# HGRN2 attention and a GELU block on one core: the first unit's steps in another order, with a new plan behind them

## The chip, the cores and the metric

The kernel runs on one core of a Trainium2 chip. The metric is the device time of one execution in microseconds, as the median over runs. All data are float32.

## The reference

```python
# q, k, v, f_logit: (4, 8, 768, 48)
f = 1.0 / (1.0 + np.exp(-f_logit))
for t in range(S):
    state = f[:, :, t, :, None] * state + np.einsum('bhd,bhe->bhde', k[:, :, t], v[:, :, t])
    y[:, :, t] = np.einsum('bhd,bhde->bhe', q[:, :, t], state)
x = y.transpose(0, 2, 1, 3).reshape(B * S, H * D)     # (3072, 384)
h = x @ w_in                                          # (3072, 2048)
g = h * (1.0 / (1.0 + np.exp(-1.702 * h)))
return g @ w_out                                      # (3072, 384)
```

A gated linear recurrence over 768 tokens for 32 heads of 48 features is followed by a block of two dense layers.

## The kernel before

The tokens are cut into 12 units of U = 256 (three for each batch entry). `attention(n)` makes the steps of unit n; the dense layers' work for the units that are done is a list, `fill`, from which items are emitted between them. A unit is two halves (f = 1 forward, f = 0 backward: the second half is kept with its time reversed) of 128 tokens, in chunks of C = 64. The steps are these:

- `load_raw(n, j)` loads f_logit, q or k (j = 0, 1, 2) into `raw`, in four pieces for units 0 and 1. `turn` puts features on the partitions: for units 0 and 1 by products with `ident` on TensorE (L376, eight to a PSUM bank, two banks for each of f, q, k), which ScalarE copies out (L381). f goes through the sigmoid to `F`, q and k to slots of `X`: KF and KR for k, QF and QR for q.
- `begin_gates` multiplies neighbouring decays to `tot` on GpSimd (L436): decays over 2, 4, ... 64 tokens.
- Six levels, m = 1 to 32, build the masked score matrix of each chunk. At level l, `set_aside` copies k to `Kc` on ScalarE (L514), `score` multiplies (L445, 32 products), `promote` multiplies k's and then q's slots in place by the decays over m tokens on VectorE (L539, two instructions for units 0 and 1), and `evacuate` merges the scores into `A` under masks: VectorE at levels 0 to 4 (L486, L505), ScalarE at level 5 (four copies, L495). q's promotion can start only when the level's products have read q.
- `turn_k` transposes the fully promoted k (L618) and ScalarE copies it to `kn`. `load_v` loads v into `vt` (first half) and `vr` (second half); `reverse_v` reverses vr's tokens by a stream shuffle on VectorE after a load that reverses the blocks of 32.
- Part "S": `add` multiplies A by v into `y` (L555), kn by v gives `pd` (L666), and VectorE carries the state over four chunks in `st`, a product and a sum for each chunk (L691, L692). Part "W": the states times q are added to y (L713), ScalarE copies y to `yT` (L728), and DMAs bring yT into the layout `xT` that the dense layers read (`to_x`, L778 and L783).

The dense layers' products are `h` (L1127, xT times w_in, 256 tokens) and `o` (L1141). The weights come in 16 pairs of 768 KB through `fetch_weights` (L207, into one of three `bits` buffers) and are converted in four steps: a prelu on ScalarE (L239), then `a`, `s` and the write to w_in or w_out on VectorE (L235, L228, L238). Pairs 0, 1 are w_in and 2, 3 are w_out of the first four of the 16 feature blocks, pairs 4, 5 and 6, 7 those of the next four, and so on.

Until unit 2 has ended every engine takes its instructions in the written order. `opening()` writes unit 0 by hand; units 1 to 3 follow `PLAN`, one string of steps behind each part: f an item of the dense layers, c one step of a conversion, w a weight fetch, p the start of the next conversion, k (any other letter) one idle product, s another sum. `keep_up` makes such idle products (L116), whose result nothing reads. From unit 3 on TensorE and GpSimd keep the written order and a scheduler orders the other engines. A DMA's issue waits in its queue until the one eight before it has landed.

The levels in the opening, and the end of it:

```python
for l in range(NL):
    chosen[:] = [2, 3][l % 2:][:1]
    level(l)                      # here: scores, products, promote k, promote q, set_aside
    ...
turn_k(0)
turn_k(2)
for l in range(NL - 1):
    evacuate(l)
    if l == 1:
        units[0][3]()             # reverse_v
```

Of the kernel before, what the change touches and what calls it, by code (L numbers as in the profile page):

```python
# [13 lines left out]
ALU = mybir.AluOpType  # L14
# [9 lines left out]
def kernel(  # L24
# [94 lines left out]
    nc.vector.memset(ones, 1.0)  # L119
    nc.scalar.activation(ones, ones, AF.Sigmoid)  # L120
    nc.vector.memset(A, 0.0)
    nc.vector.memset(ones, 1.0)
    serial = count()
    flat_A = A.rearrange("p c f t -> p (c f t)")
    keep_up(2, 192, (flat_A[:, :P], flat_A[:, :192]))

# [41 lines left out]
    w_in = const.tile([P, NFF // 2, NK, 2 * P], F32, name="w_in")  # L168
    w_out = const.tile([P, NFF, DM], F32, name="w_out")
    k_toks = [tc.dram_tile([2, G, P // 32, 32 * NP], F32, name=f"k_tok{j}") for j in range(2)]  # L170
    D2, DR = 2 * D, P - 2 * D
# [90 lines left out]

    HOLES = {(N_FILL, 0): "ccp", (N_FILL, 1): "cwcc", (N_FILL, 2): "cwp", (N_FILL, 3): "cc", (N_FILL, 4): "cw"}

# [43 lines left out]
    def load_v(n):  # L308


        if n >= NALL:
            return
        b, s0 = n // NU, n % NU * U
        vts[n] = ld.tile([P, 2, DM], F32, tag="vt", name=f"vt_{n}", bufs=2)
        vrs[n] = ld.tile([P, DM], F32, tag="vr", name=f"vr_{n}", bufs=1)
        nc.sync.dma_start(
            out=vts[n][:, 1].rearrange("p (h d) -> p h d", h=H), in_=v[b, :, s0:s0 + HALF, :].rearrange("h p d -> p h d")
        )
        for i in range(4):
            t0 = s0 + U - 32 * (i + 1)  # L320
            nc.sync.dma_start(
                out=vrs[n][32 * i:32 * (i + 1)].rearrange("p (h d) -> p h d", h=H),
                in_=v[b, :, t0:t0 + 32, :].rearrange("h p d -> p h d"),
            )

    def reverse_v(n):

        nc.vector.stream_shuffle(vts[n][:, 0], vrs[n], list(range(31, -1, -1)))

# [8 lines left out]
    def attention(n):  # L338
# [19 lines left out]
        def turn(j, outs, fn=None, pieces=None):  # L358

            if n >= N_FILL:  # L360
                for f in (1, 0):
                    out = outs(f)
                    at, step = (0, 1) if f else (HALF - 1, -1)
                    nc.vector.transpose(  # L364
                        view(out, at, [[HALF, NP], [step, R4], [R4 * step, 32]]),
                        by_half[:, j, f].rearrange("p a (j d) -> p (a j) d", j=R4)[:, :, :32],
                    )
                if fn:
                    fn()
                return  # L370
            for j0 in pieces or range(0, R, 4):
                pt = bank([P, 4, P], f"t_{n}_{j}_{j0}")
                for jj in range(4):
                    for h in range(2):
                        x = (j0 + jj) * D
                        nc.tensor.matmul(  # L376
                            pt[h * HS:(h + 1) * HS, jj, :], lhsT=by_pair[j][:, h, x:x + HS], rhs=ident, start=True, stop=True
                        )
                for f in (1, 0):
                    at, step = (j0, 1) if f else (HALF - 1 - j0, -1)  # L380
                    nc.scalar.activation(  # L381
                        view(outs(f), at, [[HALF, NP], [R * step, 16], [step, 4]]),
                        pt.rearrange("p j (a f i) -> p f a i j", a=NP, f=2)[:, 1 - f],
                        (AF.Tanh if n > 1 else AF.Sigmoid) if fn else AF.Copy, scale=0.5 if fn and n > 1 else 1.0,
                    )
            if fn and n > 1:
                half_up()
# [19 lines left out]

        def begin():
            turn(1, lambda f: slot(query(n, f)))
            if n > N_FILL:  # L410
                load_raw(n + 1, 1)

        def begin_k(between=None):
            turn(2, lambda f: slot((KR, KF)[f]))
# [65 lines left out]

        def evacuate_one(l, c, sc):

# [8 lines left out]
            if m == 32:  # L491
# [7 lines left out]
                return  # L499
            for at, f in ((HS + m, 1), (0, 0)):  # L500
                dims = [[HALF, n_c], [2 * m, 32 // m], [1, m]]
# [22 lines left out]

        def promote(l, q_too=False):

# [4 lines left out]
            if n < N_FILL:  # L531
                nb = nb // 2
                for base, other, at, to in ((KF, KR, 0, m), (QR, QF, 0, m)):
                    f = 1 if base == KF else 0
# [9 lines left out]
            if l + 1 < NL:  # L544
                set_aside(l + 1, q_too)
# [41 lines left out]
        def open_level(l):  # L587
            if l % 2 == 0:
                lane_scores(0, 1) if l == 0 else scores("y" if l == 2 else "sc")
            by_level[l] = t["both"]  # L590
            score(l % 2, l, queries(l))
            promote(l)

        def open_evacuate(l):
            for c, sc in by_level[l]:
                evacuate_one(l, c, sc[:, :, l % 2])

# [56 lines left out]
        def _():  # L654
# [17 lines left out]
            if not n:  # L672
                units[1][0][2]()
                add()

                seen = t["py"][HS:HS + 1, 1, 0, 1, :1]
                nc.scalar.copy(seen, seen)
            if n != N_FILL - 1:
                load_v(n + 1)
# [16 lines left out]
        def _():  # L696
# [26 lines left out]
            def half(h):  # L723
                for g in range(h, NG):
                    for f in (1, 0):
                        at, step = (g * HS, 1) if f else (U - 1 - g * HS, -1)
                        to, of = (rows(h), columns(h, g)) if g else (slice(0, HS + D),) * 2
                        nc.scalar.copy(view(yT[to], at, [[U, NP], [step, HS]]), py[of, g, :, f, :])  # L728
                two = ((nc.scalar, nc.sync), (nc.sync, nc.scalar))[n] if h and n < N_FILL else (nc.sync,)
                to_x(lambda h: (yT[rows(h), :NK], lambda r, d: yT[r:r + d, NK]), xT[:, :, :U], NG, (h,), two)  # L730
# [56 lines left out]

        return (begin_f, begin, begin_k, begin_gates), parts, (open_level, open_evacuate, turn_k), lambda: reverse_v(n)

# [417 lines left out]
    def parts_of(n):  # L1207
# [103 lines left out]
    def opening():  # L1311

        begin_f, begin, begin_k, begin_gates = units[0][0]
        next_f, next_q, next_k, next_gates = units[1][0]
        level, evacuate, turn_k = units[0][2]
# [10 lines left out]
        load_v(0)  # L1326
        load_raw(1, 1)
        fetch_weights()
        fetch_weights()
        for l in range(NL):  # L1330
            chosen[:] = [2, 3][l % 2:][:1]
            level(l)
            if l in (2, 3):
                next_f((0, 4)[l - 2:][:1])
            elif l < NL - 1:
                keep_up(1)
            if l == 1:
                begin_pair(0)
                state["begin"] = 1

        nc.scalar.activation(q_end, q_end, AF.Gelu_apprx_sigmoid)
        chosen[:] = [2, 3]
        turn_k(0)
        turn_k(2)
        for l in range(NL - 1):
            evacuate(l)
            if l == 1:
                units[0][3]()
        chosen[:] = [2, 3, 2, 3]
        next_q()  # L1350
        begin_pair(1)
        state["begin"] = 2
        evacuate(NL - 1)
        units[0][1][-2][1]()
        next_gates()
        for _ in range(NOP):
            convert()
        fetch_weights()

    fill = []  # L1360
    opening()
    FIRST = 'k'
    PLAN = {
# [70 lines left out]
```

## Time and profile before

| | |
|---|---|
| median of three runs | 587.08 us (585.69, 587.08, 596.66) |
| profiled execution | 587.35 us, span 585.4 us |
| TensorE busy | 564.4 us, 96% |
| VectorE, ScalarE, GpSimd busy | 441.0, 288.8, 142.5 us |
| DMA | 60.34 MB, mean 103 GB/s |
| first `h` product of the dense layers | 38.95 us |
| xT of unit 0: first issue, last issue | 33.64, 35.62 us |
| first state product `y` (L713) of unit 1 | 62.24 us |
| first `h` product of unit 1 | 69.36 us |

Times in the trace are microseconds from the start of the span. A line of the timeline gives start, length, engine, source line, operation, written and read tiles, and in brackets the idle time before it with what ended it. A float32 product leaves two records. SPq and ACTq are the instruction queues of SyncE and ScalarE while they issue DMAs.

### The profile page before, as it was taken

The page shows a single profiled execution, that of the slowest core. Times are in us where ns is not written, and L with a number is a line of the kernel's source. Part 1 is how long each engine was busy: PE and PEld are TensorE (multiplying, and loading weights), DVE is VectorE, ACT ScalarE, POOL GpSimd, SP SyncE. Part 2 cuts the span into 40 slices and gives each one's busy share as a digit, 9 for nine tenths or more (in the row PEclk, how much of TensorE's full clock was granted, in tenths as well). Part 3 has the DMA queues.
Part 4 walks back from the last instruction along what each step waited for, and adds up shares of the span by engine and source line. Part 5 has one row for each costly group of instructions (what it writes and reads, how often), then busy time and mean ns, then how long its engine had stood idle before and what let it go on. Part 6 is the DMA issues. An engine that isn't in the chain of part 4 may idle for free.

```text
span 585.4 us, 18532 instructions
## 1 busy us (share of the span) xinstructions
PE 564.4 (96%) x7838; PEld 514.6 (88%) x7838; DVE 441.0 (75%) x697; ACT 288.8 (49%) x588; POOL 142.5 (24%) x226
## 2 busy tenths in 40 slices
PE   7899889999999999999999999999999999999997
PEld 6767667676899999999999999999999999999896
DVE  2898877986888786887796897786897786461284
ACT  4755354323543563564563564563563563652440
POOL 4020220614452602402502502502402403103000
PEclk9999999999999999999999999999999999999999
DMA  7869695833352452453542343442451211001000
GB/s 183 197 185 221 172 241 133 234 79 89 100 143 55 126 125 58 116 128 82 131 113 56 103 128 86 126 115 57 120 130 43 64 39 29 29 2 36 19 1 28
DMA packets 86771, 60.34 MB, mean 103 GB/s; under 512 B 33505, under 2 KB 78465, under 8 KB 86689
## 3 DMA queue, kind: packets, MB, share of 16 engines
q1 hardware_dynamic: 86208, 58.57, 40.0%
q8 instruction: 62, 1.02, 0.7%
q10 hardware_dynamic: 481, 0.59, 0.4%
q14 instruction: 20, 0.16, 0.1%
HBM read 45.49 MB, written 8.91 MB: 93 GB/s over the span
## 4 chain that ended last, share of the span: by engine, by line
PE 73%; DVE 10%; DMA 7%; SPq 4%; ACT 3%; issue 2%; ACTq 0%; DVEq 0%
PE h L1033 17%; PE o_Y L894 14%; PE o_Z L894 9%; PE h_y L1033 6%; PE sc L445 6%; PE o_X L894 5%; PE o_W L894 4%; DMA bits<-in_moe_w_in_dram 3%; PE h L1127 3%; PE o L1141 3%; DVE X L364 2%; PE y L713 2%; PE y L555 2%; PE sc L666 2%; DVE X L543 1%
## 5 line engine op out<-in xcount | busy, mean ns | idle before, releaser
L543 DVE TENSOR_TENSOR X<-X,tot 128x1024 f32<-128x1024 f32 x50 | 67.7, 1354 | 44.7 <-PE sc L445 38.4
L514 ACT COPY Kc<-X 128x512 f32<-128x512 f32 x72 | 48.4, 672 | 81.6 <-DVE X L543 61.2
L995 POOL TENSOR_TENSOR E<-xT 128x128 f32<-128x128 f32 (+1 forms) x36 | 16.0, 455 | 229.4 <-DMA xT<-yT 229.4
L1127 PE MATMUL h<-xT,w_in 128*128 128x256 f32 x288 | 65.9, 383 | 2.6 <-DMA xT<-yT 1.8
L1127 PEld LDWEIGHTS h<-xT,w_in 128*128 128x128 f32 x288 | 53.7, 190 | 12.3 <-issue 2.4
L1033 PE MATMUL h<-E,w_in 128*128 128x128 f32 (+1 forms) x476 | 62.8, 277 | 0.5 <-DVE g L1061 0.5
L1033 PEld LDWEIGHTS h<-E,w_in 128*128 128x128 f32 x476 | 57.4, 192 | 1.4 <-issue 0.8
L894 PE MATMUL o_Y<-T,S 128*128 128x192 f32 x320 | 57.7, 329 | 0.0
L1063 ACT ACTIVATE g<-g 128x512 f32<-128x512 f32 (+1 forms) x70 | 40.4, 590 | 27.1 <-DVE g L1061 26.8
L894 PEld LDWEIGHTS o_Y<-T,S 128*128 128x128 f32 x320 | 52.2, 190 | 0.6
L1061 DVE TENSOR_TENSOR g<-g,h 128x512 f32<-128x512 f32 (+1 forms) x58 | 36.1, 637 | 15.3 <-PE h L1033 14.4
L364 DVE STREAM_TRANSPOSE X<-raw 128x512 f32<-128x512 f32 x40 | 42.4, 1115 | 3.1 <-PE y L713 1.8
L1141 PE MATMUL o<-w_out,g 128*128 128x384 f32 x128 | 43.7, 491 | 0.1
L505 DVE COPY_PREDICATED A<-masks,sc 128x256 f32<-128x256 uint32 (+1 forms) x98 | 41.8, 505 | 0.1
L1141 PEld LDWEIGHTS o<-w_out,g 128*128 128x128 f32 x128 | 23.7, 190 | 14.9 <-ACT g L1131 0.4
L728 ACT COPY yT<-y 48x256 f32<-48x256 f32 (+1 forms) x66 | 21.1, 370 | 29.3 <-PE y L713 28.9
L391 POOL TENSOR_SCALAR F<-F 128x1024 f32<-128x1024 f32 x10 | 12.8, 1278 | 87.0 <-ACT F L394 87.0
L1052 ACT ACTIVATE g<-h 128x512 f32<-128x512 f32 (+1 forms) x52 | 28.6, 577 | 9.4 <-PE h L1033 9.0
L445 PE MATMUL sc<-X,Kc 48*64 48x64 f32 x1344 | 28.3, 220 | 3.7 <-ACT Kc L514 2.1
L445 PEld LDWEIGHTS sc<-X,Kc 48*64 48x64 f32 x1344 | 24.1, 134 | 8.0 <-ACT Kc L514 4.4
L894 PE MATMUL o_X<-w_out,g 128*128 128x192 f32 x160 | 29.6, 331 | 0.5 <-ACT o_X L858 0.5
L894 PE MATMUL o_W<-T,g 128*128 128x192 f32 x160 | 29.5, 331 | 0.0
(161 smaller groups left out, 1187.2 us busy)
## 6 DMA issues: line engine op xcount, KB each, us to landing
bits<-in_moe_w_out_dram SPq DMA_DIRECT2D x8, 768.0 KB
raw<-in_f_logit_dram SPq DMA_DIRECT2D x48, 96.0 KB
raw<-in_k_dram SPq DMA_DIRECT2D x48, 96.0 KB
bits<-in_moe_w_in_dram SPq DMA_DIRECT2D x8, 576.0 KB
raw<-in_q_dram SPq DMA_DIRECT2D x44, 96.0 KB
k_tok<-z SPq DMA_DIRECT2D x64, 64.0 KB
kt<-k_tok SPq DMA_DIRECT2D x16, 256.0 KB
out_dram<-osb SPq DMA_DIRECT2D x20, 192.0 KB
```

Source lines behind the costliest of these rows:

```text
L364: nc.vector.transpose(view(out, at, [[HALF, NP], [step, R4], [R4 * step, 32]]), by_half[:, j, f].rearrange("p a (j d) -> p (a j) d", j=R4) ...
L445: nc.tensor.matmul(t["sc"][h][g * HS:(g + 1) * HS, a, s, :], lhsT=t["Kc", l][rows(h), x:x + HS], rhs=rhs(h, a, g), start=True, stop=True,)
L505: moved = nc.vector.copy_predicated(out=view(A, c * HALF + at, dims), mask=mask.bitcast(U32), data=got)
L514: nc.scalar.copy(c.rearrange("p (n two m) -> p n two m", two=2, m=m), view(X, KF * SLOT, [[2 * m, SLOT // (2 * m)], [(KR - KF) * SLOT + m, ...
L543: nc.vector.tensor_tensor(x, x, y, ALU.mult)
L894: nc.tensor.matmul(t[name], lhsT=lhs(f), rhs=rhs(f), start=(new and i == 0), stop=(i == HF - 1), skip_group_check=True,)
L1033: nc.tensor.matmul(ph[:, t], lhsT=WA[a][:, f // 2, f % 2 * P:(f % 2 + 1) * P], rhs=E[n][b], start=(root and t == 0), stop=not goes_on, ski ...
L1052: nc.scalar.activation(to, ph, AF.Copy, scale=float(sign))
L1061: nc.vector.tensor_tensor(to, to, part, ALU.add if sign > 0 else ALU.subtract)
L1063: nc.scalar.activation(to, to, AF.Gelu_apprx_sigmoid)
L1127: nc.tensor.matmul(ph, lhsT=w_in[:, ff // 2, c, ff % 2 * P:(ff % 2 + 1) * P], rhs=xTs[n][:, c, :], start=(c == 0), stop=(c == NK - 1))
L1141: nc.tensor.matmul(t["po"], lhsT=g[ff // FG][:, ff % FG, tt * P:(tt + 1) * P], rhs=w_out[:, ff, :], start=(ff == ffs[0]), stop=(ff == ffs[ ...
```

## The change

- f of unit 0 is loaded from two queues, SyncE's and ScalarE's, and most of q from SyncE's; the first table load of ScalarE stands behind its loads. Four idle products instead of two run at the start, after a memset of a quarter of A.
- For q in unit 0 one of the two banks, and for q in unit 1 both, are copied out by VectorE instead of ScalarE.
- k's promotion runs two levels ahead of q's, and each level's masked copies stand between the promotions of later levels. Levels use other PSUM banks. `turn_k` stands before the last level.
- For units 0 and 1 v's second half is loaded as it is, in one DMA, and reversed by a product with an anti-diagonal matrix, which is built by GpSimd in a part of w_out that is written later; ScalarE copies the result to vt.
- For units 0 and 1 the state is carried by one fused instruction for each pair of heads and chunk (48 columns) instead of a product and a sum for each chunk (192 columns).
- Unit 1's turns of q and k, its f's second half and the first conversions are placed elsewhere: f's second bank ahead of unit 0's state products (L713 before, L737 after), q and k behind them. The idle products behind the first unit are gone. All DMAs to xT of units 0 and 1 are issued by SyncE. Pair 3 is fetched behind the first xT instead of ahead of it.
- The plan's strings for units 1 and 2 are other ones.

```diff
-    keep_up(2, 192, (flat_A[:, :P], flat_A[:, :192]))
+    keep_up(4, 192, (flat_A[:, :P], flat_A[:, :192]))
...
+    backwards = w_out[:, NFF - 1, :P]
+    nc.gpsimd.memset(backwards, 0.0)
+    nc.gpsimd.affine_select(out=backwards, in_=backwards, compare_op=ALU.not_equal, fill=1.0, base=1 - P, pattern=[[1, P]], channel_multiplier=1)
...
     def reverse_v(n):
-        nc.vector.stream_shuffle(vts[n][:, 0], vrs[n], list(range(31, -1, -1)))
+        if n >= N_FILL:
+            nc.vector.stream_shuffle(vts[n][:, 0], vrs[n], list(range(31, -1, -1)))
+            return
+        pt = bank([P, DM], f"v_{n}")
+        nc.tensor.matmul(pt, lhsT=backwards, rhs=vrs[n], start=True, stop=True)
+        nc.scalar.copy(vts[n][:, 0], pt)
...
+                    if n < N_FILL and j == 1 and j0 // 4 <= n:
+                        nc.vector.tensor_copy(to, got)
+                        continue
...
             if not n:
-                units[1][0][2]()
                 add()
+                begin_pair(0)
+                state["begin"] = 1
                 seen = t["py"][HS:HS + 1, 1, 0, 1, :1]
                 nc.scalar.copy(seen, seen)
-            if n != N_FILL - 1:
+                begin_pair(1)
+                state["begin"] = 2
+                chosen[:] = [3]
+                units[1][0][0]((4,))
+            if n >= N_FILL:
                 load_v(n + 1)
...
+                if n < N_FILL:
+                    for a in range(NP):
+                        copied["state"] = nc.vector.scalar_tensor_tensor(
+                            st[:, c, a], t["before"][c][:, a], D64[:, ORDER.index(f), g, a:a + 1], d[:, a], op0=ALU.mult, op1=ALU.add
+                        )
+                    continue
...
-                two = ((nc.scalar, nc.sync), (nc.sync, nc.scalar))[n] if h and n < N_FILL else (nc.sync,)
+                two = (nc.sync,)
...
                 rest = ahead()
+                if n == 1:
+                    chosen[:] = [2, 3, 2, 3]
+                    units[1][0][1]()
+                    units[1][0][2]()
+                    follow_steps(SECOND)
                 scores()
...
-        load_raw(0, 0)
+        load_raw(0, 0, (nc.sync, nc.scalar))
         load_raw(0, 2)
-        load_raw(0, 1, (nc.scalar,))
+        load_raw(0, 1, (nc.scalar, nc.sync, nc.sync, nc.sync))
+        nc.scalar.activation(ones, ones, AF.Sigmoid)
...
         begin()
+        promote(0, only=(0,))
         load_raw(1, 0)
+        load_v(0)
+        fetch_weights()
+        load_raw(1, 1)
         load_raw(1, 2)
...
+        promote(1, only=(0,))
         for l in range(NL):
             chosen[:] = [2, 3][l % 2:][:1]
             level(l)
...
+            for _ in range((0, 1, 1, 2, 2, 0)[l]):
+                pieces.pop(0)()
+            pieces += evacuate(l)
+            if l < NL - 1:
+                promote(l, only=(1,))
+            if l + 2 < NL:
+                promote(l + 2, only=(0,))
+            if l == 2:
+                next_f((0,))
+            elif l == 3:
+                reverse_v(0)
+                load_v(1)
+            elif l == 4:
+                chosen[:] = [3, 2]
+                turn_k(0)
+                turn_k(2)
...
         nc.scalar.activation(q_end, q_end, AF.Gelu_apprx_sigmoid)
...
+        while pieces:
+            pieces.pop(0)()
+        promote(NL - 1, only=(1,))
         units[0][1][-2][1]()
         next_gates()
         for _ in range(NOP):
             convert()
-        fetch_weights()
...
-    FIRST = 'k'
+    FIRST = ''
+    SECOND = 'cccc'
...
-            "cccwcccwkkkkk", "kkkcf", "cfccwf", "fcffcwffcffcf", "ffcc", "f", "cwc", "fcc", "ffcf", "pw", "fw", "ff",
-            "fffffff",
+            "wccfww", "cff", "cccf", "fccfffwfcfwfcf", "fcfc", "f", "ccwc", "fcc", "f", "pwf", "ffwf", "ff", "fffff",
...
-            "ffff", "ffffffff", "fcfcfcwffcfcfcwfffcfcfcff", "sss", "fcfcfcfffffss", "fcfcfcffffffff", "",
-            "fffffffffff",
+            "fffff", "ffcfffffff", "ffcccwffcfcwfffffccff", "fcscfss", "ffcfcffffss", "cfffccffffffff", "f",
+            "fffffffff",
```

More of the change, by code (lines that the diff above doesn't have):

```diff
@@ L119 @@
     nc.vector.memset(ones, 1.0)
-    nc.scalar.activation(ones, ones, AF.Sigmoid)
-    nc.vector.memset(A, 0.0)
-    nc.vector.memset(ones, 1.0)
+    nc.vector.memset(A[:, :2], 0.0)
+    nc.vector.memset(A[:, 2:], 0.0)
     serial = count()
     flat_A = A.rearrange("p c f t -> p (c f t)")
-    keep_up(2, 192, (flat_A[:, :P], flat_A[:, :192]))
+    keep_up(4, 192, (flat_A[:, :P], flat_A[:, :192]))
     R = U // 32
@@ L260, in convert @@
             state["done"] += 2
-    HOLES = {(N_FILL, 0): "ccp", (N_FILL, 1): "cwcc", (N_FILL, 2): "cwp", (N_FILL, 3): "cc", (N_FILL, 4): "cw"}
+    HOLES = {(N_FILL, 0): "ccp", (N_FILL, 1): "cfwcc", (N_FILL, 2): "cw", (N_FILL, 3): "cc", (N_FILL, 4): "pcw"}
     def convert_in(n, l):
@@ L318, in load_v @@
         )
-        for i in range(4):
-            t0 = s0 + U - 32 * (i + 1)
+        for i in range(4 if n >= N_FILL else 1):
+            t0, w = (s0 + U - 32 * (i + 1), 32) if n >= N_FILL else (s0 + HALF, HALF)
             nc.sync.dma_start(
-                out=vrs[n][32 * i:32 * (i + 1)].rearrange("p (h d) -> p h d", h=H),
-                in_=v[b, :, t0:t0 + 32, :].rearrange("h p d -> p h d"),
+                out=vrs[n][w * i:w * (i + 1)].rearrange("p (h d) -> p h d", h=H),
+                in_=v[b, :, t0:t0 + w, :].rearrange("h p d -> p h d"),
             )
     def reverse_v(n):
-        nc.vector.stream_shuffle(vts[n][:, 0], vrs[n], list(range(31, -1, -1)))
+        if n >= N_FILL:
[4 more added lines that the diff above has]
+        nc.scalar.copy(vts[n][:, 0], pt)
     def rows(h):
@@ L380, in turn @@
                     at, step = (j0, 1) if f else (HALF - 1 - j0, -1)
+                    to = view(outs(f), at, [[HALF, NP], [R * step, 16], [step, 4]])
+                    got = pt.rearrange("p j (a f i) -> p f a i j", a=NP, f=2)[:, 1 - f]
+                    if n < N_FILL and j == 1 and j0 // 4 <= n:
+                        nc.vector.tensor_copy(to, got)
+                        continue
                     nc.scalar.activation(
-                        view(outs(f), at, [[HALF, NP], [R * step, 16], [step, 4]]),
-                        pt.rearrange("p j (a f i) -> p f a i j", a=NP, f=2)[:, 1 - f],
+                        to, got,
                         (AF.Tanh if n > 1 else AF.Sigmoid) if fn else AF.Copy, scale=0.5 if fn and n > 1 else 1.0,
@@ L406, in begin_f, with begin, begin_k @@
                 load_raw(n + 1, 0)
-        def begin():
-            turn(1, lambda f: slot(query(n, f)))
+        def begin(pieces=None):
+            turn(1, lambda f: slot(query(n, f)), None, pieces)
             if n > N_FILL:
                 load_raw(n + 1, 1)
-        def begin_k(between=None):
-            turn(2, lambda f: slot((KR, KF)[f]))
+        def begin_k(between=None, pieces=None):
+            turn(2, lambda f: slot((KR, KF)[f]), None, pieces)
+            if pieces and max(pieces) < 4:
+                return
             if n > N_FILL:
@@ L479, in evacuate, with evacuate_one @@
                     evacuate_one(l, c, sc[:, :, s])
-        def evacuate_one(l, c, sc):
+        def evacuate_one(l, c, sc, fs=(1, 0)):
             m = LEV[l]
@@ L499, in evacuate_one @@
                 return
-            for at, f in ((HS + m, 1), (0, 0)):
+            for at, f in [((0, 0), (HS + m, 1))[f] for f in fs]:
                 dims = [[HALF, n_c], [2 * m, 32 // m], [1, m]]
@@ L523, in set_aside, with promote @@
                 )
-        def promote(l, q_too=False):
+        def promote(l, q_too=False, only=(0, 1)):
             m = LEV[l]
@@ L532, in promote @@
                 nb = nb // 2
-                for base, other, at, to in ((KF, KR, 0, m), (QR, QF, 0, m)):
+                for base, other in [((KF, KR), (QR, QF))[i] for i in only]:
                     f = 1 if base == KF else 0
@@ L543, in promote @@
                 nc.vector.tensor_tensor(x, x, y, ALU.mult)
-            if l + 1 < NL:
+            if l + 1 < NL and 0 in only:
                 set_aside(l + 1, q_too)
@@ L587, in open_level @@
         def open_level(l):
-            if l % 2 == 0:
-                lane_scores(0, 1) if l == 0 else scores("y" if l == 2 else "sc")
+            if l % 3 == 0:
+                lane_scores(0, 1)
+            else:
+                scores(("sc", "y")[l % 3 % 2])
             by_level[l] = t["both"]
-            score(l % 2, l, queries(l))
-            promote(l)
+            score(0, l, queries(l))
         def open_evacuate(l):
-            for c, sc in by_level[l]:
-                evacuate_one(l, c, sc[:, :, l % 2])
+            return [lambda x=x, f=f: evacuate_one(l, x[0], x[1][:, :, 0], (f,)) for x in by_level[l] for f in (1, 0)[l in (0, NL - 1):]]
         if n < N_FILL:
@@ L786, in to_x @@
                     at += w
-        return (begin_f, begin, begin_k, begin_gates), parts, (open_level, open_evacuate, turn_k), lambda: reverse_v(n)
+        return (begin_f, begin, begin_k, begin_gates), parts, (open_level, promote, open_evacuate, turn_k)
     HF, HC = NFF // 2, DM // 2
@@ L1314, in opening @@
         next_f, next_q, next_k, next_gates = units[1][0]
-        level, evacuate, turn_k = units[0][2]
-        load_raw(0, 0)
+        level, promote, evacuate, turn_k = units[0][2]
+        load_raw(0, 0, (nc.sync, nc.scalar))
         load_raw(0, 2)
-        load_raw(0, 1, (nc.scalar,))
+        load_raw(0, 1, (nc.scalar, nc.sync, nc.sync, nc.sync))
+        nc.scalar.activation(ones, ones, AF.Sigmoid)
+        nc.vector.memset(ones, 1.0)
         fetch_weights()
@@ L1323, in opening @@
         begin()
+        promote(0, only=(0,))
         load_raw(1, 0)
+        load_v(0)
+        fetch_weights()
+        load_raw(1, 1)
         load_raw(1, 2)
-        load_v(0)
-        load_raw(1, 1)
         fetch_weights()
-        fetch_weights()
+        pieces = []
+        promote(1, only=(0,))
         for l in range(NL):
@@ L1332, in opening @@
             level(l)
-            if l in (2, 3):
-                next_f((0, 4)[l - 2:][:1])
-            elif l < NL - 1:
+            for _ in range((0, 1, 1, 2, 2, 0)[l]):
[14 more added lines that the diff above has]
+                turn_k(2)
+            elif l < 2:
                 keep_up(1)
-            if l == 1:
-                begin_pair(0)
-                state["begin"] = 1
         nc.scalar.activation(q_end, q_end, AF.Gelu_apprx_sigmoid)
[L1342 to L1353, printed above, removed]
+        while pieces:
+            pieces.pop(0)()
+        promote(NL - 1, only=(1,))
         units[0][1][-2][1]()
@@ L1357, in opening @@
             convert()
-        fetch_weights()
     fill = []
     opening()
-    FIRST = 'k'
+    FIRST = ''
+    SECOND = 'cccc'
     PLAN = {
```

## The prediction

> **What bounds the kernel now.** I read the page from the top. TensorE (PE) is busy for 96% of the span and in nearly every slice but the first; so the question is what it does there and how much of the rest is waiting.
>
> ```profile
> span 585.4 us, 18532 instructions
> PE 564.4 (96%) x7838; PEld 514.6 (88%) x7838; DVE 441.0 (75%) x697; ACT 288.8 (49%) x588; POOL 142.5 (24%) x226
> PE   7899889999999999999999999999999999999997
> ```
>
> The timeline of the first 40 us shows that the early busy time is not the work that counts. The lines are start, length, engine, line and operation:
>
> ```profile
> 2.02 1.65 PE L116 MATMUL idle<-A 128*128 128x192 f32 x4 [2.02 <-DVE A L121]
> 4.72 6.93 PE L376 MATMUL t<-ident,raw 128*64 128x128 f32 x96 [1.05 <-DMA raw<-in_f_logit_dram]
> 12.64 0.70 PE L445 MATMUL sc<-X,Kc 48*64 48x64 f32 x32 [1.00 <-ACT X L381]
> 14.34 0.70 PE L445 MATMUL sc<-X,Kc 48*64 48x64 f32 x32 [0.26 <-DVE X L539]
> 15.94 0.69 PE L445 MATMUL sc<-X,Kc 48*64 48x64 f32 x32 [0.17 <-DVE X L539]
> 20.54 1.28 ACT L1341 ACT_TABLE_LOAD   x1
> 27.27 1.50 ACT L495 COPY A<-sc 32x256 f32<-32x256 f32 x4
> 31.57 0.38 SPq L207 DMA_DIRECT2D bits<-in_moe_w_out_dram  x1
> 32.32 1.96 ACT L728 COPY yT<-y 112x256 f32<-112x256 f32 x6 [1.28 <-PE y L713]
> 33.64 0.61 SPq L778 DMA_DIRECT2D xT<-yT  x1
> 38.95 1.24 PE L1127 MATMUL h<-xT,w_in 128*128 128x256 f32 x5
> ```
>
> Until 38.95 us a latency chain of unit 0 decides: loads, turns, six score levels, masked copies, state, y, yT, xT. The MLP's first product h starts there. From then on PE is the bound: the waits of PE between 36 and 180 us are few and short.
>
> ```profile
> PE sc L445 <- ACT Kc L514: 2.1, 2, 1.2
> PE h L1127 <- DMA xT<-yT: 1.8, 1, 1.8
> PE h L1127 <- ACT g L1131: 0.8, 1, 0.8
> PE sc L445 <- DVE A L505: 0.6, 1, 0.6
> ```
>
> So the time is (start of the first h) + (PE work behind it) + (some 5 us of waits before 180 us, and a tail the change doesn't touch). An edit counts by how it moves each of the three. The profiled execution took 587.35 us, 0.27 above the median of 587.08 and 1.95 above its span; sums are made against 587.35.
>
> **The change, part by part.**
>
> *Loads and the first turns.* f goes out on SP and ACT, two pieces each. The last of four pieces was issued at 2.12 and landed at 4.58; now the last is issued at about 1.2, and pieces landed 2.1 to 2.5 us after issue: 3.3 to 3.7. PE has four idle products ahead instead of two and starts them at 1.36, since only a quarter of A's 0.91 us memset is waited for; at 0.32 us a record they end near 4.1, so the turns begin there (4.72 before). The speed of the turns is read from PE's timeline in two stretches:
>
> ```profile
> 4.72 2.62 PE L376 MATMUL t<-ident,raw 128*64 128x128 f32 x22 [1.05 <-DMA raw<-in_f_logit_dram]
> 9.28 2.37 PE L376 MATMUL t<-ident,raw 128*64 128x128 f32 x40
> ```
>
> A pair of records is spaced 0.213 us in the first and 0.109 in the second; the single records put the step at 7.77, 3.05 us after 4.72 and 5.75 us after the first idle product. Counted from 1.36 it would come at 4.4 to 7.1; at worst it stays at 7.77. I take 5.8: eight cold pairs, forty fast ones, the 48 turns end at 10.15 instead of 11.6. The Trainium skill (TensorE: Matmul & The Clock Gate, part 1) says that PE runs at half clock until one free-running window of about 3.4 us was busy; this trace agrees in kind (0.213 to 0.109), and by the page's window and a free phase I estimate the step between 4.8 and 8.2. On ACT, F, K and Kc follow the turns; one of q's two turns is now copied by DVE, which is idle there, so that after Kc (ends 10.25) only one X pair (0.66) is left: first scores at about 11.2 instead of 12.64. Bounds 10.85 (k's loads land no earlier than 6.4) to 12.05 (step at 7.77).
>
> *Promotions and masked copies.* Per level the chain was score 0.70, q promotion 0.69, two hand-overs: 1.60 to 1.65. It stays, and K promotions and A copies fill DVE's gap. At a rate of 0.61 a promotion and 0.33 a masked copy the gap (1.60 - 0.61 = 0.99) holds K and one half A copy (0.95), but not K and two copies (1.27). And q's first promotion now stands behind K1, which waits for Kc1. Written out: scores at 11.2, 13.35, 15.15, 16.8, 18.6; the k turns (1.09) are put before the last, at 20.45 (20.84 before). So the levels lose 1.1 of the 1.45 us. In return the twelve masked copies and the shuffle (22.2 to 26.65, after the last level) are gone from the chain except some 1.9 us behind the last q promotion, under sc and pd.
>
> *v reversed by a product.* 0.68 us on PE by the rows of o (128x384), 0.48 on ACT by the copy of o; SP issues one load in place of four (0.45 each). In the opening PE waits there anyway, if vr has landed: it is issued at about 8.8 behind one weight pair and f of unit 1, lands at 15 to 17.5, and is needed at 17.4. POOL's memset and select for the matrix (0.20 + 0.30 by ident's rows) lie in its idle time before 8.9.
>
> *State and masked ACT copies.* kn is copied by 21.05; the table load (1.28) and q_end, which before lay at 20.54, come next and hold back the four A copies of L495: 22.6 to 24.1 (27.27 to 28.76 before). State: twelve fused steps of 128x48. No row shows one; bounds are 0.13 each (masks, 128x64, one every 0.105) and 0.25 (384 columns take 0.62). 1.6 to 3.0 us against 2.37, hidden beside the A copies and y.
>
> *From A to yT.* ACT now has prelu, the y copy (after y, 1.3 behind A), prelu 0.94, a second table load 1.28, F's two sigmoids 0.66, and only then yT: 4.5 us where it was 3.56. y_X on PE ends about 1 us sooner than that, so ACT decides. yT at 28.6 instead of 32.32. The Trainium skill (ScalarE: Activation LUTs, What ACT_TABLE_LOAD costs) puts a switch at 1.28 plus a drain of 1.38. The trace differs: the copy before the load ended at 20.52, the load ran 20.54 to 21.82, the next activation began at 21.83. By the rule the two switches on the path would, as an estimate, cost 2.8 us more; I go by the row.
>
> *xT.* Six issues in a row on SP (0.6 each) instead of four there and two on ACT: 1.2 us later in issue, but weight pair 3 (768 KB, issued 31.57) is no longer ahead of them. 6.63 us from yT to h before; I take 6.7: h at **35.3 instead of 38.95, -3.65** (-2.4 to -4.3).
>
> *PE work behind the first h.* Unit 1's second score level (0.69) moves behind it, and the second reversal (0.68) is new: **+1.35**. The dropped idle products lay in front of h.
>
> *Unit 1's state, y and stream.* h_7 and an o that covered the state chain (pd ends 59.5, y_X at 62.24) are moved; one o (0.68) is left over a chain of 1.6 to 3.0 us for three of its four chunks' steps. And on DVE pair 7's conversion now stands ahead of the state. y_X then waits 0 to 1.2: **+0.6**. xT of unit 1 loses its ACT queue (+0.6) but has seven o behind y_X instead of six (+0.68): zero. The new plan puts two o ahead of the score that waited 0.59 for A: **-0.3** (0 to -1.8, if the 1.2 us wait on Kc goes too).
>
> Sum: -3.65 + 1.35 + 0.6 - 0.3 = **-2.0**: 585.35 for such an execution, **585.1 us** against the median. With all bounds: -4.8 to +0.15, so 582.3 to 587.2.
>
> **The rivals.**
> (1) More gained: clock early, and the waits on Kc and A both covered by the plan. -4.8 to -6: about 582. For it: DVE's transposes for unit 2 start earlier, since pair 7 is done before. Against: K1 before q's first promotion, ACT's extra load.
> (2) No gain: late clock (-0.85 lost) and y_X waiting its full 1.2 us: 587.
> (3) Slower, by the weight stream. Pair 3 is issued behind six xT loads, near 33.2 instead of 31.57, and pairs 4 to 7 and unit 2's raw loads stand behind it on SP. Before, pair 7 landed at 55.54; now ACT's second kn copy stands behind its prelu and the state behind its conversion. If it lands 1.7 us later than before, y_X of unit 1 is no earlier than before and the gain is gone; 3 us later gives 1.2 us more plus the 0.6 of SP's issues: 589. Against it: slots come free earlier, and xT's 0.39 MB no longer lies inside the stream.
> (4) PE cools. The idle products that filled PE between 32.8 and 38.9 are gone; I reckon gaps of 1.9 and 1.5 us around the one score level there. Back at 0.213 for 0.109 over 3.05 us, the first h lose 1.5 us: 586.6. A gap of 1.27 (11.37 to 12.64) left the pace fast, so I give it little. The skill's same page puts the limit at an idle window of about 3.4 us, which none of these gaps reaches.
>
> **How the numbers follow.** Forecast 0.52, more gained 0.15, no gain 0.13, weights late 0.13, PE cools 0.07. The range 581.9 to 588.8 holds the forecast's bounds, rival 1's better half and most of rival 3. 2% (11.7 us) is about what a measurement of this kernel can tell from no change, its three runs lying between 585.69 and 596.66; no case reaches it, as the opening would have to lose a third. I leave 0.02 for faster and 0.03 for slower beyond it.
>
> **What would show it.** Right: first scores near 11, fourth level near 17, L495's successor ending near 24, a table load straight before F and yT, first yT near 28.6, h near 35.3 without a long DMA wait, PE's waits after 36 us still 4 to 6 us, y_X of unit 1 waiting for the state. Wrong: h after 37; the reversal waiting for vr; a second slow stretch of PE; pair 7's prelu or conversion named before unit 1's state; PE's waits before 130 us above 8 us.

## The result and the profile after

The changed kernel takes **591.31 us** (median of 4 runs, 590.72 to 591.52) against 586.87 for the kernel before in the same session (585.69 to 596.66). The ratio, which leaves out the slow execution of 596.66 us, is 1.0081, 95% interval 1.0061 to 1.0101: 0.8% slower, a little under 5 us. The forecast was 585.1 us, range 581.9 to 588.8. The time lies outside it, on the other side of the kernel before.

The page of the profiled execution (591.23 us; the kernel before had 587.35). Each digit is a 40th of the span:

```profile
span 589.4 us, 18517 instructions
PE   7789899699999999999999999999999999999997
PEclk9989999889999999999999999999999999999999
```

The span is 4.0 us longer. There is one new dent, in the eighth digit of PE (103 to 118 us), and two places where the granted clock falls: near 29 us and from 115 us on. The opening, from the timeline (start, length, engine, line, operation; in brackets the idle time before it and what ended it):

```profile
4.43 5.97 PE L383 MATMUL t<-ident,raw 128*64 128x128 f32 x96 [0.28 <-DMA raw<-in_f_logit_dram]
11.15 0.70 PE L458 MATMUL sc<-X,Kc 48*64 48x64 f32 x32 [0.75 <-ACT X L393]
22.90 1.49 ACT L508 COPY A<-sc 32x256 f32<-32x256 f32 x4
28.05 0.27 PE L383 MATMUL t<-ident,raw 128*64 128x128 f32 x1 [1.59 <-issue]
29.27 5.64 PE L383 MATMUL t<-ident,raw 128*64 128x128 f32 x64
29.48 1.95 ACT L752 COPY yT<-y 112x256 f32<-112x256 f32 x6 [0.47 <-PE y L737]
36.54 0.70 PE L458 MATMUL sc<-X,Kc 48*64 48x64 f32 x32 [1.63 <-ACT Kc L527]
37.17 1.56 PE L1151 MATMUL h<-xT,w_in 128*128 128x256 f32 x6
```

Up to the A copies (22.90) everything stands where the prediction put it. Then PE stops for 1.59 us with no releaser ("issue"), the 64 products of the turns take 5.64 us, and the first h comes at 37.17: 1.78 us sooner than before, not 3.65. It is still sooner. The loss is elsewhere, and the three largest of PE's waits from 30 to 180 us name it (total, times, longest):

```profile
PE o L1165 <- DVE sum L1217: 4.4, 1, 4.4
PE sc L458 <- ACT Kc L527: 1.8, 2, 1.6
PE h L1151 <- DMA xT<-yT: 1.3, 1, 1.3
```

The same place in the profile of before, where PE does not wait:

```profile
99.34 0.91 ACT L239 ACTIVATE bits<-bits 128x768 f32<-128x768 f32 x1
111.04 0.60 PE L618 MATMUL tkn<-ident,X 128*128 128x128 f32 x4
111.47 6.62 PE L1141 MATMUL o<-w_out,g 128*128 128x384 f32 x20
```

PE's timeline at the wait, then DVE's, in the profile of after:

```profile
110.72 0.60 PE L631 MATMUL tkn<-ident,X 128*128 128x128 f32 x4
115.76 8.29 PE L1165 MATMUL o<-w_out,g 128*128 128x384 f32 x16 [4.44 <-DVE sum L1217]
```

```profile
102.65 0.56 DVE L230 TENSOR_SCALAR s<-bits 128x768 int32<-128x768 int32 x1 [4.15 <-ACT bits L241]
108.18 3.98 DVE L832 TENSOR_TENSOR T<-w_out 128x768 f32<-128x768 f32 x2
112.08 1.63 DVE L237 TENSOR_SCALAR a<-bits 128x768 int32<-128x768 uint32 x1
113.63 1.62 DVE L230 TENSOR_SCALAR s<-bits 128x768 int32<-128x768 int32 x1
115.17 0.54 DVE L1217 TENSOR_TENSOR sum<-sum,o 128x384 f32<-128x384 f32 x1
```

At the turn of k at 110.72 the changed kernel is ahead. Both kernels have 32 o to do around the two turns; here 16 are left, before there were 20 at 111.04. That is 0.32 us and four o of 0.34: 1.7 us ahead. Then PE stands still for 4.44 us, because the next o needs a PSUM bank that DVE's sum at 115.17 frees. The sum is late because DVE waited 4.15 us for ACT's prelu of pair 13 (L241, at 101.71; in the kernel before 99.34) and everything behind it moved. After the stop the 16 o take 8.29 us; 16 o at full clock take 5.43 (the second run below). So 4.44 + 2.86 = 7.3 us are lost. The span is 4.0 us longer: -1.7 + 7.3 - 1.6. The last term is a net one: a wait of 0.82 us at 127.6 and one of 0.90 at 246.7, which the kernel before has and the changed one has not, and some 0.4 us in the tail, whose cause stays open, less 0.5 us more of waiting near 175 us.

The clock by stretches of the changed kernel (window, its length, busy time with count of PE, PEld, DVE, ACT, POOL; granted clock; DMA share; GB/s). The trace puts the steps at 5.51, 29.41, 32.82, 114.74 and 121.56:

```profile
26.00:29.40 3.40, 1.81 (x60) 1.30 (x57) 2.61 (x8) 2.43 (x4) 0.25 (x1) 1.00 0.03 8
29.41:32.81 3.40, 3.40 (x34) 3.40 (x35) 0.76 (x2) 1.91 (x6) 2.55 (x6) 0.50 0.18 41
111.33:114.73 3.40, 0.00 (x0) 0.00 (x0) 3.40 (x3) 1.38 (x2) 3.32 (x3) 1.00 1.02 210
114.74:121.55 6.81, 5.79 (x9) 3.21 (x10) 6.71 (x10) 0.00 (x0) 1.55 (x2) 0.50 0.13 30
```

All steps are multiples of 3.413 us apart. Behind the window with PE idle, and behind the one with PE idle for nearly half of it, the next one runs at half clock.

### The profile page after: what moved, and what is told of

It reads as the page before. It is cut to its first block, busy times and chain, and to the rows that moved or that the text cites. A ratio compares the mean times of both kernels' runs of the same rounds, so it can differ in the third digit from the quotient of the medians.

```text
span 589.4 us, 18517 instructions
## 1 busy us (share of the span) xinstructions
PE 566.0 (96%) x7826; PEld 515.9 (88%) x7826; DVE 442.6 (75%) x714; ACT 289.9 (49%) x586; POOL 140.4 (24%) x228
## 4 chain that ended last, share of the span: by engine, by line
PE 72%; DVE 12%; DMA 6%; issue 4%; SPq 3%; ACT 2%; DVEq 0%; ACTq 0%
PE h L1057 15%; PE o_Y L918 13%; PE o_Z L918 8%; PE h_y L1057 6%; PE sc L458 5%; PE o_X L918 5%; PE o_W L918 4%; PE h L1151 4%; PE o L1165 3%; DVE X L371 2%; PE t L383 2%; DMA raw<-in_q_dram 2%; PE y L737 2%; PE y L568 2%; DVE X L556 2%
## 5 line engine op out<-in xcount | busy, mean ns | idle before, releaser
L1165 PE MATMUL o<-w_out,g 128*128 128x384 f32 x128 | 46.9, 518 | 4.4 <-DVE sum L1217 4.4
L1165 PEld LDWEIGHTS o<-w_out,g 128*128 128x128 f32 x128 | 25.0, 201 | 20.5 <-DVE sum L1217 4.7
L1155 ACT ACTIVATE g<-h 128x256 f32<-128x256 f32 x48 | 17.3, 385 | 31.1 <-PE h L1151 30.9
```

What stands on the lines that cost most here:

```text
L1165: nc.tensor.matmul(t["po"], lhsT=g[ff // FG][:, ff % FG, tt * P:(tt + 1) * P], rhs=w_out[:, ff, :], start=(ff == ffs[0]), stop=(ff == ffs[ ...
```

## The experiments

**Theory.** The new plan of unit 2 puts two conversion steps ("c") behind five h. ACT's prelu then stands behind their gelus, DVE behind the prelu, and PE, 14 us later, behind DVE. **Rivals:** the PSUM banks now come round in an order in which an o needs a bank sooner; DVE's subtractions of w_out quarters, not needed yet, stand ahead of the sum; the weight stream is late; ACT's two more table loads spoil the opening. The first four runs below take up the banks, the plan's steps, the subtractions and the table loads. The weight stream has no run of its own: pair 13's prelu starts with no wait for a DMA, straight behind a gelu, and the run with the two steps put ahead loses the wait with every load in its place. The change also sets the steps between unit 2's score levels anew (the table `HOLES`); every run on the changed kernel keeps that table. The kernel before had a median of 587.52 us in their session.

**One o behind the turn of k again (e1).**

```
-  "ffcccwffcfcwfffffccff", "fcscfss", "ffcfcffffss",
+  "ffcccwffcfcwfffffccff", "fcscss", "fffcfcffffss",
```

> One step of the written plan of unit 2 is moved: the single o product that stood ahead of the first turn of k goes behind it, as in the kernel before. Theory A (the order of PSUM banks): the o of the next row block no longer is the first to need the bank of the first o; the turn's bank comes first, freed early by ACT, and one whole o (1.36 us) lies in front of the wait. PE's wait at 111 us then falls from 4.4 to about 3.1 us, and if that is short enough for the clock to stay up, the slow stretch behind it (2.9 us) goes too: 587 to 590. Theory B (DVE's late sum alone decides, banks only shift the wait): the o that waits stands elsewhere, the wait is still 4 us or more, 590.5 to 592. Rival C (the loss is not at 111 us but in the weight stream): no change at all, 591.3.

Measured: 587.37 us, ratio to before 1.0006 (0.9984 to 1.0028). The wait for the sum is 1.84 us and a second one of 1.42 stands at the next h; the prelu is as late as ever relative to PE: 6.95 us behind the first h of that stretch, as in the changed kernel (3.07 in the kernel before). (The profiled execution was the slowest of ten, 592.22, with two more slow clock windows.) The bank order carries part of the loss.

**The two conversion steps ahead of the five h (e2).**

```
-  "ffcccwffcfcwfffffccff",
+  "ffcccwffcfcwccfffffff",
```

> The two conversion steps that the plan of unit 2 put behind five h are put ahead of them. Theory A (ACT's prelu of pair 13 stands behind the gelus and holds DVE): the prelu is back near 99.4 us (101.7), DVE's 4.15 us wait for it shrinks to about 1.8, the transposes start near 101.5 and the first sum ends near 113.4 instead of 115.7; PE's wait falls to about 2.1 us, too short for a slow clock: 585.5 to 588. If the wait still cools PE: about 589. Theory B (DVE's subtractions of 2 us each and its steps beside POOL decide, the prelu is hidden): wait 3.5 us or more, 590 to 592.

Measured: **585.76 us**, ratio to before **0.9977** (0.9962 to 0.9992). DVE and PE of this run:

```profile
98.99 0.55 DVE L230 TENSOR_SCALAR s<-bits 128x768 int32<-128x768 int32 x1
104.07 1.80 DVE L832 TENSOR_TENSOR T<-w_out 128x768 f32<-128x768 f32 x2
111.39 0.54 DVE L1217 TENSOR_TENSOR sum<-sum,o 128x384 f32<-128x384 f32 x1
```

```profile
111.28 0.60 PE L631 MATMUL tkn<-ident,X 128*128 128x128 f32 x4
111.99 5.43 PE L1165 MATMUL o<-w_out,g 128*128 128x384 f32 x16
```

The s step comes 3.7 us sooner, the sum 3.8 us, and PE does not wait. It does better than expected, since the subtractions now run before POOL's sums begin (1.80 us for two, not 3.98). This one string is worth 5.5 us by the medians (5.7 by the spans of the profiles), and this version is faster than both kernels, by 0.2% against before: 1.4 us by the ratio, 1.8 by the medians.

**The subtractions behind the sum (e5).** The conversion steps stay late.

```
+  copied[n, r, tt] = nc.vector.tensor_tensor(acc, acc, po, ALU.add)
...
+  with tc.issue_after(copied[0, 2, 0].ins):
+      sub(T[1][:, x], quarter(w_out, 0, 1, x), quarter(w_out, 0, 0, x))
```

> DVE's two halves of the first subtraction of w_out quarters (1.95 us each, not needed before unit 3) are issued behind the sum of the first o instead of ahead of it; nothing else changes. Theory A (PE waits for the sum because DVE is late, whatever made it late): the sum ends near 111.8 instead of 115.7, PE's wait falls from 4.4 to below 0.8, the clock stays up: 4 + 2.9 us less, 584 to 585.5. Theory B (DVE's order only moves the wait to the next sums, since the four us of subtractions then stand ahead of those): one to two us of wait each at the following o, 587 to 590. Rival C (weights late): 591.

Measured: 587.26 us, ratio 1.0008 (0.9992 to 1.0023). The wait shrinks to 0.54 us, but 1.42 us come back at the next h, behind the sums that the subtractions now precede. Theory B of the expectation: delayed work on DVE moves the wait on.

**Without the preload of the Gelu table (e3).**

```
-  nc.scalar.activation(q_end, q_end, AF.Gelu_apprx_sigmoid)
```

> Left out: the Gelu of four dummy columns of q_end in the opening, with the table load that it causes (21.50) and the one that brings the first table back (26.51); q_end is overwritten later, so the output is the same. Theory A (ACT's extra loads hold the chain of the opening): the A copies of ACT start near 21.5 instead of 22.9, F's turn and y come 1.3 to 2.6 us sooner, yT near 27 to 28 instead of 29.5, the first h near 34.5 to 36 instead of 37.2; PE's gaps of 0.87 and 1.59 us go if they belong to the loads; 1 to 2.5 us less: 588.5 to 590.5. Theory B (the gaps are instruction fetch or the state chain): first h within 0.5 us of 37.2, 591 plus or minus 0.5. With the window near 26 to 29.4 busier, the slow clock at 29.4 to 32.8 should go by A and stay by B.

Measured: 591.76 us, ratio 1.0082 (1.0057 to 1.0106): no change from the changed kernel's 591.31. The A copies start at 22.23 (21.5 was expected), but PE's stop grows:

```profile
28.77 0.37 PE L383 MATMUL t<-ident,raw 128*64 128x128 f32 x1 [2.95 <-issue]
```

So neither the table loads nor ACT make the stops. They lie at the same places of PE's program. Counting PE's weight loads, products and waits, it goes on with instructions 706 and 962 in the changed kernel, in e2 and in this run; later stops, in e8 and e10, end at 1474 and 1986: 256, 512 and 512 apart. In the trace a 16 KB packet of the instruction queue lands 1.3 to 1.6 us before PE goes on: 21.63 and 26.77 in the changed kernel (PE at 23.06 and 28.05), 27.31 in this run (PE at 28.77). No view names a releaser; from the places and the packets I read that PE is out of code there.

**The same lateness in the kernel before (e9).** Order of banks and o untouched:

```
-  "fcfcfcwffcfcfcwfffcfcfcff",
+  "fcfcfcwffcfcfcwffffffcccf",
```

> The kernel before, with one pair's conversion steps of unit 2 put three to four h later, as the changed kernel has them; its order of turns and o is untouched, so four o lie between the first use of a PSUM bank and its next. Theory A (late prelu and bank order both count): the prelu comes 2 us later, the first sum ends near 115.9 instead of 113.9, PE needs it near 114.2 and waits about 1.7 us, too short for a slow clock: 588.5 to 589.5. Theory B (the bank order decides, the late prelu is covered without it): no wait, 587.0 to 587.8. Theory C (the late prelu alone makes the whole loss): wait of 4 us and a slow clock, 591 to 594.

Measured: 592.06 us, ratio 1.0078 (1.0060 to 1.0097). The prelu came not 2 but 5.5 us later (104.87), since the gelus ahead of it keep PE's pace of 1.3 us. Relative to PE that is the lateness of the changed kernel: 7.06 us behind the first h of the stretch (6.95 there). DVE's wait for it, and PE's for the sum:

```profile
105.80 0.56 DVE L228 TENSOR_SCALAR s<-bits 128x768 int32<-128x768 int32 x1 [3.69 <-ACT bits L239]
```

```profile
PE o L1141 <- DVE sum L1193: 2.8, 1, 2.8
```

With the old banks the wait is 2.8 us and no slow window follows; with the new it was 4.4 and one did. So the late step makes the wait in either kernel, and e2 shows that without it there is none; e1 shows that the bank order makes it worse. The 2.8 us and 0.7 more of waiting for g are less than the 4.7 of the medians; in this profile the opening is also 1.2 us later, from a clock step at 9.34 us. The rest is not attributed.

**The opening: idle products in the stop (e6),** on top of e2 as all that follow; the kernel before had 587.33 us in the session of e6 to e9.

```
+  keep_up(4)
   units[1][0][0]((4,))
```

> On top of the conversion steps put ahead (the run that took away the wait at 111 us): four idle products of 128x320 (1.6 us) in front of the last turn of f of unit 1, where PE stood still for 1.6 to 1.8 us and a slow clock window of 3.41 us began near 29. Theory A (that window is granted by how busy the window before it was, and PE's half pace holds the turns of k): no slow window near 29, the 64 products of the turns take 4.4 instead of 5.4 us, the score behind Kc stands near 35.7 and the first h near 36.3 to 36.7 instead of 37.3; 0.7 to 1 us less: near 585. Theory B (the standstill is in the fetch of instructions and the idle products are only more code): they run before the stop, the stop stays and ends at the same time, the clock still holds. Theory C (the products themselves delay y): first h 37.5 to 38.5, 586 to 587.

Measured: 588.86 us, ratio to before 1.0024 (1.0011 to 1.0037). Theory A holds for the clock: no slow window near 29, the turns take 4.01 us, the first h is at 36.50. But the time grows by 3.1 us against e2. The gain is not passed on at unit 1, and more is lost later:

```profile
70.46 6.89 PE L1153 MATMUL h<-xT,w_in 128*128 128x256 f32 x24 [2.73 <-DMA xT<-yT]
171.81 1.49 PE L679 MATMUL sc<-vt,kn 64*64 64x48 f32 x64 [2.48 <-ACT kn L654]
```

PE now waits 2.73 us for unit 1's xT (1.70 in e2), and a slow window follows at 70 us. That xT lands 0.5 us later than in e2, although y is 0.5 us earlier, is not settled; the weight pair ahead of it on SP is issued 0.25 us later. Between 127 and 163 us e6's h products lie only 0.9 us behind e2's, from 204 us on 3.9 us: the rest comes at 171.81, where PE waits 2.48 us (1.13 in e2) for ACT's copy of a later unit's k, which waits 2.35 us for its DMA (0.97 in e2), and a slow window follows at 172.4. Why that DMA is later is not shown.

**The third weight pair late (e7).**

```
   load_raw(1, 2)
-  fetch_weights()
...
+  FIRST = 'w'
```

> On top of the conversion steps put ahead: the third weight pair (768 KB) is issued only after the opening instead of at 19.5 us. Theory A (PE's stops at 22.2 and 26.4 us, which the profile puts down to no releaser, are its next 16 KB of instructions, queued behind the weights): the instruction packet that started at 25.3 us starts near 23.6 and lands near 24.7, and the second stop shrinks from 1.8 us to below 0.5; the first (packet at 19.9, ahead of the moved load) stays. The pair then lands late and the total may grow by 1 to 3 us. Theory B (the stops have to do with ACT or the state): both stay within 0.3 us of 0.9 and 1.6 to 1.8.

Measured: 588.29 us in one execution. The stop is 2.10 us (1.83 in e2) and the packet lands at 28.28 (PE at 29.60). So that pair does not hold the packet; what sets its time stays open.

**Unit 1's v by the shuffle (e8).**

```
-  if n >= N_FILL:
+  if n >= 1:
       nc.vector.stream_shuffle(vts[n][:, 0], vrs[n], list(range(31, -1, -1)))
```

> On top of the conversion steps put ahead: unit 1's v is reversed by DVE's shuffle and four loads again, as in the kernel before; unit 0 keeps the product. Theory A (PE is the bound there, the product costs its 0.68 us): 0.5 to 0.7 us less, near 585.1. Theory B (DVE is late for unit 1's scores and state, the shuffle's 0.65 us comes back as a wait of PE for A, Kc or the state): same or up to 0.7 us more, 585.8 to 586.5.

Measured: 588.09 us, ratio 1.0017 (0.9996 to 1.0038), neither theory. It showed something else: its profile has no slow window near 29, since its free-running windows begin at 4.26 us, and then the first h comes at 35.42:

```profile
35.42 1.56 PE L1151 MATMUL h<-xT,w_in 128*128 128x256 f32 x6
```

Yet unit 1's first h stands at 69.41, as in the changed kernel (69.44) and before (69.36), after a wait of 2.48 us. In e2 it stands at 69.97, after 1.70 us. A slow window at 69.1 takes the 0.56 us that are left of the opening's gain. At 163 us this run is level with e2 (0.06 us ahead), as theory B has it; the 2.5 us that its profile is longer come behind that, from a wait of 2.04 us at 170.4, again for the copy of k, and the slow window that follows it.

**Can unit 1's xT be had sooner (e10 to e13)?** A weight pair of 768 KB is issued 1 to 4 us ahead of it. e10 is e6 with the pair behind xT; e11 is e6 with the second half of xT on two queues; e12 has both; e13 is both without the idle products. The kernel before had 587.49 us.

```
-  "ccwc", "fcc", "f", "pwf",
+  "ccc", "fcc", "f", "wpwf",
...
-  two = (nc.sync,)
+  two = (nc.sync, nc.scalar) if h and n == 1 else (nc.sync,)
```

> The conversion steps put ahead and the four idle products (588.9 us), and now the weight pair that SP issues 1.4 us ahead of unit 1's xT goes behind it; the orders of PE, ACT and DVE stay. Theory A (the gain of the opening was lost at unit 1's xT, whose six transfers queue behind that pair and landed 5.3 to 3.1 us after issue): they land 1.8 to 2.6 us after issue, as unit 0's do; SP's last issue is near 67.6, so the h there starts near 69.4 instead of 70.46, PE waits 1.7 instead of 2.7 us and a slow window near 70 becomes rarer: 585.5 to 587.5. The pair lands 5 us later and may show as a wait on Kc or a sum between 72 and 95 us, 0 to 2 us. Theory B (SP's own six issues set the time, the pair is harmless): wait still 2.4 to 2.7, 588.5 to 589.5.

> The conversion steps put ahead and the four idle products, and unit 1's second half of xT is issued half on SP and half on ACT again, as the kernel before has it; the weight pair stays ahead. Theory A (the pair ahead holds xT): the transfers land where they did, 69.7 to 70.7, wait 2.3 to 2.7 us, 588.3 to 589.3. Theory B (six issues in a row on SP hold it): the last issue comes 0.6 us sooner, wait near 2.1, slow window rarer: 587 to 588.3.

> Both: the pair behind xT and the second half of xT on two queues, with the conversion steps ahead and the idle products. If A and B each hold a part: last issue near 67, landed near 68.9, h at 68.9 to 69.1, PE waits 1.1 to 1.4 us, seldom a slow window: 584.7 to 586.5. If the pair's late landing comes back as waits behind 72 us: 586.5 to 588.

> The conversion steps ahead, the pair behind xT and the second half on two queues, but no idle products in the opening: the slow window near 29 is back and the first h is 0.8 us later. If the first h still sets the time once xT is early: 0.5 to 0.9 us more than with the idle products, 585.5 to 587. If unit 1's xT still decides (its wait takes up what the opening gains): the same within 0.3 us, with PE's wait there 0.8 us shorter.

Measured: 598.39, 592.34, 595.98 and 594.16 us; ratios 1.0180 (1.0146 to 1.0214), 1.0082 (1.0054 to 1.0109), 1.0146 (1.0113 to 1.0180) and 1.0115 (1.0082 to 1.0149). All four expectations were wrong. In e10 xT's transfers do land 1.8 to 2.7 us after issue and PE waits 1.4 us for them, though unit 1's first h is no earlier (70.61). But DVE then waits 5.0 us for the pair, and PE for DVE:

```profile
81.67 2.93 PE L1151 MATMUL h<-xT,w_in 128*128 128x256 f32 x6 [6.93 <-DVE sum L1217]
```

In e11 SP's third issue of xT, after the one that went to ACT's queue, stands until 69.15, just after ACT's transfer landed at 69.13, and all of xT is later. In e12 and e13 too PE waits for DVE's sum, 6.75 and 4.65 us. The pair and xT want the same microseconds; either order costs, and of those tried the one in place is the cheaper.

## Why the prediction was wrong, point by point

**The step that failed: the new plan of unit 2 was not costed.** The sum was made of the opening, of unit 1 and of two waits near 80 us; the stretch from 95 to 130 us stands in it at zero, without a reason, and "PE's waits before 130 us above 8 us" stood only among the signs of error (behind 36 us they came to 7.9). Two others of those signs did come: the first h after 37 us (37.17) and a second slow stretch. No term followed a moved "c" from ACT's queue to DVE's to a PSUM bank. What the runs showed in its place is a wait of 4.44 us and 2.86 us of slow clock behind it; the chain is worth 5.5 us by e2.

**That e2 then comes out 1.4 to 1.8 us below the kernel before, where -2.0 was forecast, is luck.** By the sum unit 1's first h would have come 1.7 us sooner than before; in e2 it comes 0.61 later (69.97). What e2 gains comes behind it, from waits that the sum had at -0.3 or not at all: those at 76.7 and 83.4 us, and those at 127.6 and 246.7 us.

**Loads, first turns, promotions, A copies: right.** Turns at 4.43 (4.1 said), clock step 5.51 (5.8), first scores 11.15 (11.2), last score level 20.86 (20.45), A copies 22.90 to 24.39 (22.6 to 24.1), the reversal at 17.32 without a wait for vr.

**yT and the first h: mis-sized, -3.65 against -1.78.** The prediction held that PE's y_X ends a microsecond before ACT is ready. PE stopped for code there, y_X ended at 29.35, and yT came at 29.48 instead of 28.6: 0.88 of the 1.87 us that are missing. The other 0.99 lie between yT and h (7.69 us, where 6.7 was taken for xT's path): the slow window stretched the turns of k, and not xT but the score that stands ahead of the first h, waiting for their Kc, held it. In e8 and e13, without the window, the first h is at 35.42 and 35.84 where 35.3 was forecast. So PE cooled, as rival 4 has it (chance 0.07), and at about its price: the first h is 1.3 to 1.8 us later than in those two runs, where it had 1.5. But the place is another: it had the gaps beside a score level that the dropped idle products leave behind 32.8 us, and the window there (PE busy for 2.06 of 3.41 us) has full clock behind it; the slow window lies at 29.41, behind the stop for code. Its reason to be unlikely, a gap of 1.27 us that had left the pace fast, does not carry over. In these traces the clock steps only at multiples of 3.41 us from its first step, so a single gap does not decide: in the kernel before the window of that gap has PE busy for 2.15 us, here 1.81 at 26 us.

The Trainium skill (TensorE: Matmul & The Clock Gate, part 1) has the window of about 3.4 us, free-running, and these steps agree (3.413 us); it lets the clock fall after an idle window, and here one with PE busy for 1.81 of 3.40 us was enough.

**Work behind the first h (+1.35) and y_X's wait (+0.6, measured 0.34): the terms are there, the sum is not complete.** The added score level (32 products) and the reversal are as counted. But from the first h to the wait for unit 1's xT PE needs 2.30 us more than before (30.93 against 28.63), not 1.69; 0.6 us stay open. A wait for xT that is 0.44 shorter (1.34 against 1.78) hides most of that, and unit 1's first h moves by -1.78 + 2.30 - 0.44 = +0.08.

**xT of unit 1 ("zero"): the term that hides the opening.** In e6 a first h 0.84 us sooner than in e2 becomes 0.49 later at unit 1, in e8 one 1.92 sooner becomes 0.56 sooner.

**Waits behind it (-0.3, bound -1.8): at its bound.** The waits of 1.21 and 0.59 us that the kernel before has at 76.7 and 83.4 us are gone, 0.17 is left. In e2 the products gain 1.56 us between unit 1's first h and 96 us, while what the opening gains does not even pay for the added work (+0.61 at unit 1).

**Rivals.** The slower one (weights late, 589) has the right price and the wrong place: none of PE's waits in the changed kernel goes back to a late pair, but e10 shows what one 5 us late would cost. None of the rivals had a conversion step late by plan.

## What to carry over

In a plan written out by hand, follow every moved step through each in-order queue to the buffer it frees, not only in the stage the edit is about: here two letters moved behind five others cost 5.5 us, 14 us later and two engines on. Where one buffer order gives a bank a whole product less of slack, a late engine shows at once; put optional work behind the instruction that frees the bank, but repair the lateness first. And an earlier start counts only as far as the next transfer that doesn't move with it.

## What the runs showed of the hardware

**PE can run out of code.** In stretches of many short products PE stopped for 0.3 to 2.95 us at places a multiple of 256 instructions apart, though not at every one, until 1.3 to 1.6 us after a 16 KB instruction packet landed. The Trainium skill (Runtime: NRT & Kernel Launch, Instruction fetch mechanics) describes blocks of 256 instructions and 16 KiB, which agrees, and calls the cost of a boundary mostly hidden, which here it is not.

**DVE beside POOL.** DVE's conversion steps of 128x768 took 1.63 and 1.62 us while POOL's sums (L980) ran and 0.55 without; its subtractions 1.99 against 0.95. In e2 the subtractions ran before POOL's sums and took 0.90 each; its conversion steps beside them still took 1.30 and 1.62.

**The clock turns a wait of a certain length into more.** 4.44 us of waiting cost 2.86 on top, and near 70 us waits of 1.90 to 2.97 us were each followed by one slow window, waits of 1.28 to 1.81 by none. Idle time alone does not tell: e2's window at 66.68 us has PE busy for 1.71 of 3.41 us and full clock behind it, the changed kernel's at 26 us 1.81 and half clock. The first step lies between 4.04 and 9.34 us in these profiles, so the windows fall differently in each execution: in the ten runs of e2 the mean clock was 1.000, 0.997 or 0.994, and the times went from 584.24 to 588.36 us.
